# A fourth output buffer, and the last output bank copied in two halves

## The chip, the core and the metric

The kernel runs on one core of a Trainium2 chip. The metric is device time in microseconds (us), lower is better. TensorE (PE) multiplies matrices and writes into the accumulator memory PSUM, which has eight banks; VectorE (DVE), ScalarE (ACT) and GpSimd (POOL) do the elementwise work out of the on-chip buffer SBUF; SyncE (SP) issues all DMA transfers, in program order.

## The reference

A block-causal attention, then two gated feed-forward layers, the second of them fed by the first:

```python
attn = softmax(mask(q @ k.T / sqrt(64))) @ v          # 4 batches, 8 heads, 576 tokens, 64 wide
x = attn, heads joined                                # 2304 x 512
h = maximum(maximum(x @ w1, x @ w2), x @ w3)          # 2304 x 768
x = h @ w_out                                         # 2304 x 512
gate = sigmoid(x @ w_gate); val = x @ w_val           # 2304 x 1536 each
out = (gate * val) @ w_out2                           # 2304 x 512
```

## The kernel before

Each operand of a product is split into a high and a low part, and a product is three matmuls (high x high, high x low, low x high). Attention and layer one run first, interleaved by a planner, and write their result to a DRAM tensor `x2d`. Layer two then runs in three chunks `c` of 768 tokens. A chunk loads its part of `x2d` as `xraw` (L1107), forms seven combinations of its blocks (differences `t`, L1117; high parts `xc` cast on ScalarE, L1121; low parts subtracted by VectorE, L102), and multiplies them with seven combinations of weights by a Strassen-like scheme: seven products per block `n` of 128 hidden columns.

The weights of a block come in three parts, `x`, `y` and `z`, each loaded as `wr` (L1156), cast to its high part `wgx`, `wgy`, `wgz` on ScalarE (L1160), and subtracted to its low part on VectorE or GpSimd (L102). In chunk 0 the low part is also stored (`lowp`, L1167) for the later chunks. The products of a block (L1221 to L1223) go to three accumulator banks a, b, c in the order 0 (a), 5 (b), 4 (c), then 1 (a again, on `wgz`) and so on. Between product 0 and product 1, ScalarE copies bank a to `p1`, which VectorE adds to other products; product 1 then adds into that bank.

After twelve blocks, the output matmuls (L1275 to L1277) fill six banks per chunk, 128 tokens each. `leave(c, i)` copies bank `i` to an output buffer `osb` (ScalarE L93, VectorE L97, in the pattern A, A, V) and stores it. There are three output buffers, so bank `i` uses the buffer of bank `i - 3` and waits for its store.

What sets the order: the code gives each step a time `t` and a scheduler places the instructions of DVE, ACT, POOL and SP, by these and by when data and buffers become ready; PE's order is written out. The buffers of layer two reuse the memory of the phases before: the pools are laid one behind the other from the start of SBUF. A tile must then wait for the last use of whatever lay at its addresses. Layer one's pools, from the same start, are XT (26,624 B per partition), `raw` (four buffers of 4,096 B, weight preparation), `tmp` (four of 2,048 B, the running maximum `m`, L543 and L545), and so on. Layer two's pools begin like this:

```python
    wr_p = pool("wr", 4)      # 4 x 3,072 B
    hidden(2)                 # 2 x 6,144 B
    ost_p = pool("ost", 3)    # 3 x 2,048 B
    xr_p = pool("xr", 1)      # xraw, 12,288 B
    pt_p = pool("pt", 17)
```

Of the kernel before, what the change touches and what calls it, by code (L numbers as in the profile page):

```python
# [23 lines left out]
TOK = B * S  # L24
# [54 lines left out]
def block_attention_moe_moe(ctx: ExitStack, tc, kq1, v1, kq2, vt, wa, wb, out):  # L79
    nc = tc.nc  # L80
    wide = wa.dtype == U64
    V, A, G, T = nc.vector, nc.scalar, nc.gpsimd, nc.tensor
# [8 lines left out]
    def copy(e, out, in_, scale=None):  # L91
        if e == "A":
            A.activation(out, in_, AF.Copy, scale=scale) if scale is not None else A.copy(out, in_)  # L93
        else:
            n = V if e == "V" else G
            if scale is None:
                n.tensor_copy(out, in_)  # L97
            else:
                n.tensor_scalar(out=out, in0=in_, scalar1=scale, scalar2=None, op0=ALU.mult)  # L99
# [962 lines left out]
    def pool(name, bufs, **kw):  # L1062
        return ctx.enter_context(tc.tile_pool(name=name, bufs=bufs, reuse_waits="tile", **kw))

    HC = 2 * N2
    HID = []

    def hidden(n):
        p = pool(f"hid{len(HID)}", 1)
        HID.extend(p.tile([128, 2, HC], F32R, name=f"hid{len(HID) + k}") for k in range(n))  # L1070
# [7 lines left out]

    wr_p = pool("wr", 4)
    hidden(2)  # L1080
    ost_p = pool("ost", 3)
    xr_p = pool("xr", 1)
    pt_p = pool("pt", 17)
    wg_p = pool("wg", 2)
# [123 lines left out]
    WG, OW, OUTB, LAST, ASKED = {}, {}, {}, {}, {}  # L1208
# [71 lines left out]
    def leave(c, i):  # L1280
        def g():
            o = ost_p.tile([128, 512], F32, tag="ost", name="osb")
            copy(ENG["oc"][i % 3], o, OUTB[c, i])
            r0 = HC * c + 128 * i
            nc.sync.dma_start(out=out[r0 : r0 + 128, :], in_=o)
        return g

# [139 lines left out]
```

## Time and profile before

| | us |
|---|---|
| median of 3 runs | 893.38 |
| lowest and highest | 892.27 and 895.14 |
| the profiled execution, its own time | 895.03 |
| its span, first to last instruction | 892.9 |
| TensorE busy | 870.0 |
| VectorE, ScalarE, GpSimd busy | 582.0, 446.0, 96.4 |

All times in the rows below count from the span's start. Busy times of TensorE overlap a little, since matmuls are pipelined. The span is the time from the first to the last instruction; what lies around it is 2.1 us.

### The profile page before, as it was taken

How to read it: one execution, taken by the hardware profiler on the slowest of the kernel's cores; microseconds unless marked ns; L12 is line 12 of the kernel's file. 1: busy time of each engine (PE TensorE's matmuls, PEld its weight loads, DVE VectorE, ACT ScalarE, POOL GpSimd, SP SyncE). 2: the span in 40 equal slices, each digit the busy share in tenths (PEclk: the TensorE clock that was granted, in tenths of full speed). 3: DMA queues.
4: the chain of work that ended last, by engine and by line, in shares of the span. 5: the costliest groups of instructions: out<-in, count | busy, mean ns of one | idle time of the engine just before them, and what ended most of it. 6: DMA issues, size and time to landing. Idle time of an engine off the chain costs nothing.

```text
span 892.9 us, 15107 instructions
## 1 busy us (share of the span) xinstructions
PE 870.0 (97%) x5432; PEld 789.6 (88%) x5432; DVE 582.0 (65%) x1367; ACT 446.0 (50%) x1014; POOL 96.4 (11%) x91
## 2 busy tenths in 40 slices
PE   5899999999999999999999999999999999999997
PEld 4688889887998898889999999889999988999986
DVE  7999959996799699698354778821555711555400
ACT  7897646553464355345224655512566622565311
POOL 0000000000000000000002544200222300232300
PEclk9999999999999999999999999999999999999999
DMA  9921254346534444626317988744789844788232
GB/s 334 377 82 46 74 182 145 111 141 210 193 103 142 148 135 139 207 88 223 112 35 233 323 256 296 294 156 150 249 268 305 296 131 139 249 257 286 93 106 82
DMA packets 82810, 165.09 MB, mean 185 GB/s; under 512 B 10800, under 2 KB 23600, under 8 KB 82736
## 3 DMA queue, kind: packets, MB, share of 16 engines
q1 hardware_dynamic: 82736, 164.14, 55.6%
q8 instruction: 42, 0.69, 0.3%
q14 instruction: 32, 0.26, 0.1%
HBM read 126.35 MB, written 37.75 MB: 184 GB/s over the span
## 4 chain that ended last, share of the span: by engine, by line
PE 85%; DMA 7%; DVE 3%; SPq 2%; issue 1%; ACT 1%; POOL 1%; ACTq 0%; POOLq 0%; DVEq 0%
PE ps_m L535 9%; PE ps_m L537 8%; PE ps_m L536 8%; PE acc L1221 7%; PE acc L1222 7%; PE acc L1223 7%; PE acc L1276 5%; PE acc L1277 5%; PE acc L1275 5%; PE ps_o L488 5%; PE ps_t L452 4%; PE ps_s L376 3%; PE ps_m L574 2%; PE ps_m L576 2%; PE ps_m L575 2%; DMA qk<-in_kq_dram 2%
## 5 line engine op out<-in xcount | busy, mean ns | idle before, releaser
L535 PE MATMUL ps_m<-XT,w 128*128 128x320 f32 (+2 forms) x504 | 163.6, 325 | 2.7 <-DVE x2s L97 2.6
L537 PE MATMUL ps_m<-XT,w 128*128 128x320 f32 (+2 forms) x504 | 157.9, 313 | 0.3 <-DVE w L102 0.3
L536 PE MATMUL ps_m<-XT,w 128*128 128x320 f32 (+2 forms) x504 | 157.8, 313 | 0.1
L535 PEld LDWEIGHTS ps_m<-XT,w 128*128 128x128 f32 x504 | 95.0, 188 | 10.7 <-issue 3.5
L537 PEld LDWEIGHTS ps_m<-XT,w 128*128 128x128 f32 x504 | 94.9, 188 | 3.4 <-DVE w L102 0.5
L536 PEld LDWEIGHTS ps_m<-XT,w 128*128 128x128 f32 x504 | 95.1, 189 | 2.7 <-DVE XT L102 0.3
L400 ACT ACTIVATE E<-ps_s,nm 128x256 f32<-128x256 f32 (+3 forms) x128 | 66.4, 527 | 39.1 <-PE ps_t L452 31.2
L1277 PE MATMUL acc<-ow,hid 128*128 128x512 f32 x216 | 84.1, 390 | 0.0
L1276 PE MATMUL acc<-ow,hid 128*128 128x512 f32 x216 | 84.1, 390 | 0.0
L1275 PE MATMUL acc<-ow,hid 128*128 128x512 f32 x216 | 84.0, 389 | 0.0
L1223 PE MATMUL acc<-xc,wgx 128*128 128x384 f32 x216 | 72.2, 334 | 0.0
L1221 PE MATMUL acc<-xc,wgx 128*128 128x384 f32 x216 | 72.2, 334 | 0.0
L1222 PE MATMUL acc<-xc,wgx 128*128 128x384 f32 x216 | 72.2, 334 | 0.0
L97 DVE COPY osb<-acc 128x512 f32<-128x512 f32 x6 | 4.2, 692 | 95.8 <-PE acc L1277 88.8
L1189 ACT CAST ow<-or 128x512 fp32r<-128x512 f32 x36 | 22.4, 621 | 77.7 <-PE acc L1277 55.1
L1234 DVE TENSOR_TENSOR u<-acc,p 128x384 f32<-128x384 f32 x72 | 39.9, 554 | 30.3 <-PE acc L1223 22.9
L545 DVE TENSOR_TENSOR m<-ps_m,m 128x320 f32<-128x320 f32 (+2 forms) x84 | 41.7, 496 | 23.3 <-PE ps_m L537 21.9
L395 DVE TENSOR_REDUCE nm<-ps_s 128x1 f32<-128x256 f32 (+3 forms) x128 | 55.0, 472 | 2.2 <-ACT E L400 2.2
L452 PE MATMUL ps_t<-ident,E 128*128 128x128 f32 x320 | 45.6, 281 | 7.8 <-DVE E L99 4.2
L102 POOL TENSOR_TENSOR wgx<-wr,wgx 128x768 fp32r<-128x768 f32 x1 | 1.9, 1854 | 468.1 <-ACT wgx L1160 468.1
L1234 DVE TENSOR_TENSOR u<-acc,u 128x384 f32<-128x384 f32 x72 | 40.0, 556 | 16.7 <-PE acc L1223 15.5
L1221 PE MATMUL acc<-xc,wgy 128*128 128x384 f32 x144 | 48.6, 337 | 1.8 <-DVE u L1234 1.7
(122 smaller groups left out, 2080.4 us busy)
## 6 DMA issues: line engine op xcount, KB each, us to landing
praw<-in_wb_dram SPq DMA_DIRECT2D x36, 512.0 KB, 4.7
wr<-pairs SPq DMA_DIRECT2D x72, 256.0 KB, 3.7
wr<-pairs SPq DMA_DIRECT2D x36, 384.0 KB, 4.5
or<-outs SPq DMA_DIRECT2D x36, 256.0 KB, 3.5
wgx<-lowp SPq DMA_DIRECT2D x24, 384.0 KB, 4.0
wland<-in_wa_dram SPq DMA_DIRECT2D x5, 1536.0 KB, 16.4
qk<-in_kq_dram SPq DMA_DIRECT2D x16, 480.0 KB, 3.4
wgz<-lowp SPq DMA_DIRECT2D x24, 256.0 KB, 4.2
```

Source lines behind the costliest of these rows:

```text
L400: A.activation(E[h][:, e : e + 128 * (t + 1)], j.s[h, t], AF.Exp, bias=j.nm[:, c : c + 1], scale=1.0, accum_out=j.sm[:, c : c + 1],)
L452: T.transpose(ps[:, 128 * i : 128 * i + 128], E[h][:, e : e + 128], ident)
L535: T.matmul(ps, wt[:, 0, w, k], xh[:, k], start=(k == 0), stop=False)
L536: T.matmul(ps, wt[:, 0, w, k], xl[:, k], start=False, stop=False)
L537: T.matmul(ps, wt[:, 1, w, k], xh[:, k], start=False, stop=(k == KD - 1))
L1221: T.matmul(ps, w[:, 0, h], x[:, 0, h], start=start and h == 0, stop=False, skip_group_check=True)
L1222: T.matmul(ps, w[:, 0, h], x[:, 1, h], start=False, stop=False, skip_group_check=True)
L1223: T.matmul(ps, w[:, 1, h], x[:, 0, h], start=False, stop=h == 1, skip_group_check=True)
L1234: V.tensor_tensor(out=o, in0=BK[c, n, b][:, :N2], in1=x, op=ALU.add)
L1275: T.matmul(ps, h[:, 0, ct], w[:, 0], start=(f == 0), stop=False)
L1276: T.matmul(ps, h[:, 0, ct], w[:, 1], start=False, stop=False)
L1277: T.matmul(ps, h[:, 1, ct], w[:, 0], start=False, stop=(f == NF2 - 1))
```

## The change

The pool of output buffers gets a fourth buffer. For the last bank of the last chunk, the copy is made in two halves of 256 columns, the first on ScalarE and the second on VectorE, each with a store of its own in place of one store of 512 columns.

```diff
-    ost_p = pool("ost", 3)
+    ost_p = pool("ost", 4)
...
     def leave(c, i):
         def g():
             o = ost_p.tile([128, 512], F32, tag="ost", name="osb")
+            r0 = HC * c + 128 * i
+            if c + 1 == TOK // HC and i == 5:
+                for e, k in (("A", 0), ("V", 256)):
+                    copy(e, o[:, k : k + 256], OUTB[c, i][:, k : k + 256])
+                    nc.sync.dma_start(out=out[r0 : r0 + 128, k : k + 256], in_=o[:, k : k + 256])
+                return
             copy(ENG["oc"][i % 3], o, OUTB[c, i])
-            r0 = HC * c + 128 * i
             nc.sync.dma_start(out=out[r0 : r0 + 128, :], in_=o)
```

The order in which the instructions stand changes in the middle of the program too. On SyncE, where layer one ends and layer two begins (numbers in names are those of the buffers' tiles, `x2d` stores are the last results of layer one):

```order
-L1107 DMA xraw_5940<-x2d_72 128x4x768
 L595 DMA x2d_72<-x2s_5453 128x128
 L595 DMA x2d_72<-x2s_5453 128x64
@@ -220,4 +219,5 @@
 L1156 DMA wr_5945<-pairs0_73 128x768
 L1156 DMA wr_5949<-pairs0_73 128x512
+L1107 DMA xraw_5940<-x2d_72 128x4x768
 L1156 DMA wr_5953<-pairs0_73 128x512
 L1156 DMA wr_5967<-pairs1_74 128x768
```

The load of `xraw` has moved from among the stores of an earlier group to behind the first two weight loads of layer two.

On ScalarE at the same place, before (`m` and HR belong to layer one, `wgx_5960`, `wgz_5965` and `wgy_5974` to block 0, `wgx_5989`, `wgz_5993` and `wgy_5999` to block 1):

```order
L558 CAST HR_730<-m2_5781 128x320
L1160 CAST wgx_5960<-wr_5945 128x768
L1160 CAST wgz_5965<-wr_5949 128x512
L1160 CAST wgy_5974<-wr_5953 128x512
L1121 CAST xc6_5902<-t3_5985 128x768
L1160 CAST wgx_5989<-wr_5967 128x768
L1305 COPY p1_6014<-acc_6005 128x384
L1246 ACTIVATE c11_6049<-acc_6005 128x384
L1160 CAST wgz_5993<-wr_5976 128x512
```

and of the change:

```order
L1121 CAST xc1_5928<-xraw_5940 128x768
L1160 CAST wgx_5960<-wr_5945 128x768
L1160 CAST wgz_5965<-wr_5949 128x512
L1160 CAST wgy_5974<-wr_5953 128x512
L1121 CAST xc2_5930<-xraw_5940 128x768
L1121 CAST xc3_5929<-t4_5969 128x768
L1160 CAST wgx_5989<-wr_5967 128x768
L1160 CAST wgz_5993<-wr_5976 128x512
L1121 CAST xc6_5902<-t3_5985 128x768
L1160 CAST wgy_5999<-wr_5982 128x512
L1310 COPY p1_6014<-acc_6005 128x384
```

All `xc` casts have moved from among layer one's work to behind the last HR cast (`warm`, `xc0`, `xc4` and `xc5` stand just ahead of these rows), and the copy to `p1` now stands behind the casts of `wgz_5993` and `wgy_5999`, which were behind it. On SyncE the load for `wgy_5999` is `wr_5982`; it stands behind the store of the low part of `wgz_5965`.

At the end of VectorE's program, with what each instruction waits for (DMAHW: a transfer; PE, Activation, DVE: that engine), before:

```order
L97 COPY osb_9730<-acc_9459 128x512 [waits DMAHW5_49,PE_49]
L97 COPY osb_9748<-acc_9494 128x512 [waits DMAHW7_49,DVE_49,PE_49]
```

and of the change:

```order
L97 COPY osb_9730<-acc_9459 128x512 [waits DMAHW3_49,DMAHW4_49,DMAHW0_49,PE_49]
L97 COPY osb_9748<-acc_9494 128x256 [waits DMAHW6_49,DMAHW3_49,Activation_49]
```

The last copy is half as wide, and waits for ScalarE where it waited for TensorE.

## Rows read from the trace of the kernel before

**Rows 1.** The page, part 1: TensorE's busy time and share.

```profile
PE 870.0 (97%) x5432; PEld 789.6 (88%) x5432; DVE 582.0 (65%) x1367; ACT 446.0 (50%) x1014; POOL 96.4 (11%) x91
```

**Rows 2.** Waits of PE from 476 us on: total us, times, longest.

```profile
PE acc L1221 <- DVE u L1234: 1.7, 3, 1.2
```

**Rows 3.** Timeline of PE at the seam: start, us, engine, instruction.

```profile
475.62 0.31 PE L576 MATMUL ps_m<-HR,w 128*128 128x320 f32 x1
475.76 0.34 PE L1221 MATMUL acc<-xc,wgx 128*128 128x384 f32 x1
...
478.89 0.33 PE L1221 MATMUL acc<-xc,wgz 128*128 128x384 f32 x1
```

**Rows 4.** Timeline of SP's issues, 405 to 482 us.

```profile
427.76 0.54 SPq L1107 DMA_DIRECT2D xraw<-x2d  x1
...
465.40 1.74 SPq L1156 DMA_DIRECT2D wr<-pairs  x4
...
478.32 0.38 SPq L1156 DMA_DIRECT2D wr<-pairs  x1
...
479.82 0.48 SPq L1156 DMA_DIRECT2D wr<-pairs  x1
```

**Rows 5.** Tile `xraw`: its three loads, issue to landing.

```profile
DMA to landing us min/median/max: 7.3/8.7/9.4
```

**Rows 6.** Timeline of DVE, 440 to 465 us (brackets: idle before, releaser).

```profile
440.43 0.95 DVE L1117 TENSOR_TENSOR t<-xraw 128x768 f32<-128x768 f32 x1
...
463.71 0.49 DVE L545 TENSOR_TENSOR m<-ps_m,m 128x320 f32<-128x320 f32 x1 [2.08 <-PE ps_m L537]
```

**Rows 7.** Timeline of ACT, 468 to 485 us.

```profile
468.53 0.83 ACT L1160 CAST wgx<-wr 128x768 fp32r<-128x768 f32 x1 [2.14 <-DMA wr<-pairs]
...
477.06 0.48 ACT L1305 COPY p<-acc 128x384 f32<-128x384 f32 x1 [4.46 <-PE acc L1223]
...
481.55 0.62 ACT L1160 CAST wgz<-wr 128x512 fp32r<-128x512 f32 x1 [0.93 <-DMA wr<-pairs]
...
484.44 0.62 ACT L1160 CAST wgy<-wr 128x512 fp32r<-128x512 f32 x1 [1.33 <-DMA wr<-pairs]
```

**Rows 8.** Timeline of POOL at the seam.

```profile
469.45 1.85 POOL L102 TENSOR_TENSOR wgx<-wr,wgx 128x768 fp32r<-128x768 f32 x1 [468.15 <-ACT wgx L1160]
471.26 1.30 POOL L102 TENSOR_TENSOR wgz<-wr,wgz 128x512 fp32r<-128x512 f32 x1
```

**Rows 9.** Timeline of POOL, 703 to 710 us.

```profile
703.20 1.02 POOL L102 TENSOR_TENSOR hid<-u,hid 128x384 fp32r<-128x384 f32 x1 [2.31 <-issue]
...
707.92 1.73 POOL L102 TENSOR_TENSOR hid<-u,hid 128x384 fp32r<-128x384 f32 x1
```

**Rows 10.** Timeline of DVE, the same stretch.

```profile
707.12 1.66 DVE L1117 TENSOR_TENSOR t<-xraw,t 128x768 f32<-128x768 f32 x1
```

**Rows 11.** The page, part 6: loads, KB each, median us to landing.

```profile
wr<-pairs SPq DMA_DIRECT2D x72, 256.0 KB, 3.7
```

**Rows 12.** PE by stretch: us, busy (x), granted clock, DMA share, GB/s.

```profile
21.00:21.50 0.50, 0.41 (x2) 0.50 1.06 418
...
24.00:24.50 0.50, 0.50 (x6) 0.95 1.03 410
```

**Rows 13.** Timeline of PE after a gap early on.

```profile
21.09 1.54 PE L452 MATMUL ps_t<-ident,E 128*128 128x128 f32 x6 [2.21 <-ACT E L93]
```

**Rows 14.** Timeline of ACT at the end.

```profile
887.66 1.29 ACT L93 COPY osb<-acc 128x512 f32<-128x512 f32 x2 [1.48 <-PE acc L1277]
```

**Rows 15.** Timeline of DVE at the end.

```profile
889.14 0.69 DVE L97 COPY osb<-acc 128x512 f32<-128x512 f32 x1 [2.18 <-DMA out_dram<-osb]
```

**Rows 16.** Timeline of PE at the end: the last matmul.

```profile
887.89 0.39 PE L1277 MATMUL acc<-ow,hid 128*128 128x512 f32 x1
```

**Rows 17.** ACT by line and shape: count, busy us, mean ns, idle before.

```profile
L543 ACT COPY m<-ps_m 128x256 f32<-128x256 f32 x12 | 4.5, 374 | 1.7 <-PE ps_m L537 1.7
```

**Rows 18.** DVE by line and shape.

```profile
L97 DVE CAST XT<-ps_o 128x256 fp32r<-128x256 f32 x10 | 4.2, 420 | 0.3 <-PE ps_o L488 0.3
```

## The prediction

> **What bounds the kernel now.** I first read the totals of the page and the engines' shares: TensorE is busy for 870.0 of the 892.9 us [rows 1], so only what delays TensorE, or follows its last matmul, counts. Then the waits of TensorE from 476 us on: all that is left there is 1.7 us in three waits [rows 2]. From the seam between the two layers to the end TensorE thus has almost no slack, and a delay at the seam reaches the end nearly whole. The change touches two places, the tail and, by way of the memory layout, the seam.
>
> The seam in TensorE's timeline: its last matmul of layer one starts at 475.62, the first product of layer two follows at 475.76 with no gap, and the fourth product (the first on `wgz`) starts at 478.89 [rows 3]. In SyncE's timeline the load `xraw` is issued at 427.76, 48 us ahead, and four `wr` loads at 465.40 [rows 4].
>
> **The memory layout.** In the code, `xraw` begins at 26,624 B (XT) plus the room left after it: `wr` 12,288 + two hidden tiles 12,288 + three output buffers 6,144 = 30,720, and ends at 43,008. That is exactly where the four raw buffers of layer one (4 x 4,096 after XT) end. With a fourth output buffer it begins and ends 2,048 higher and so also covers the first of layer one's `tmp` buffers, which holds a maximum `m`. The order excerpts show what follows: the load is now issued behind the first two `wr` loads. The buffer's last reader is a max that starts at 463.71 [rows 6]; the `wr` loads in front wait for the last matmul on XT and start at 465.40.
>
> **The price of the seam, step by step.** T is the time at which `xraw` has landed.
>
> 1. Four issues take 1.74 us [rows 4], so the third stands at 465.40 + 2 x 0.435 = 466.3. From issue to landing it took 7.3, 8.7 and 9.4 us [rows 5]. With 640 KB of loads in front and as much behind I take the middle row: T = 475.0 (bounds 473.6 and 475.7).
> 2. ScalarE, before, had done the `xc` casts long ahead and cast the weights at once (468.53). Now `warm` and the casts of `xc0`, `xc4`, `xc5` and `xc1` stand in front of `wgx`, and all of these need `xraw`. `warm` and `xc0` lie beside VectorE's first difference, which takes 0.95 [rows 6] and which `xc4` needs; from there come four casts of 0.83, the duration of the weight cast of the same size [rows 7], the last being `wgx`: T + 4.3.
> 3. GpSimd subtracts for `wgx` and then `wgz`: 1.85 + 1.30 = 3.15 us when alone [rows 8]. Before, VectorE was nearly idle then; now it makes its row of `xc` subtractions at the same time. Later in the kernel, where both do that, a GpSimd subtraction of 384 columns takes 1.73 instead of 1.02 [rows 9], and a VectorE one 1.66 [rows 10] instead of 0.95. I take the factor 1.7, since this is the same pair of instructions: 5.35 us, T + 9.65. Bounds: 3.15 and 5.35.
> 4. SyncE stores the low part of `wgz`, and only then issues the load `wr` for `wgy` of the second block: its issues are 0.5 apart (three steps from 478.32 to 479.82 [rows 4]), T + 10.15.
> 5. The load lands 3.7 us later by the page's median for 256 KB [rows 11]; bounds 3.2 (478.32 to 481.55) and 4.6 (479.82 to 484.44) [rows 4, 7]. T + 13.85.
> 6. ScalarE casts it (0.62) and only then copies `p1` (0.48) [rows 7], which stands behind it in its order now and stood ahead of it before. T + 14.95. The fourth product adds into the bank that this copy reads, so it waits for it, and all of TensorE behind it.
>
> The first three products are hidden in this: they need `wgx` from GpSimd (T + 4.3 + 1.85 x 1.7 = T + 7.4) and take 3.1 us. The fourth starts at 475.0 + 14.95 = 489.95 in place of 478.89: **+11.1 us**. The second block's `p1` copy stands behind one more load, for the third block's `wgz`. That is issued when the second block's low parts have been stored, some 1.0 us after step 5, at about T + 14.9; with 3.7 + 0.62 + 0.48 the copy is done at T + 19.7. TensorE wants it six products later, at T + 14.95 + 6 x 1.04 = T + 21.2 (1.04 is a third of the 3.13 us between the first and the fourth product [rows 3]). Nothing is added, with 1.5 us in hand.
>
> The Trainium skill, "SBUF — State Buffer" (section on the two separate sides of SBUF), says that a VectorE instruction with two SBUF inputs and a GpSimd one reading SBUF take a shared port by turns, whole instruction by whole instruction. By it GpSimd's two subtractions would each wait for one VectorE instruction, an estimate of 3.15 + 2 x 0.95 = 5.05 against 5.35 by the rows; the sum would be 0.3 lower.
>
> **The clock.** TensorE now stands still before the first product, before its third matmul, and for some 4.5 us before the fourth product. At the start of the kernel, behind a gap of 2.21 us that ends at 21.09, the granted clock is at half (1.2 of 2.4 GHz), and it is back just after 24.0 [rows 12, 13]: 2.95 us of work at half speed, 1.5 us lost. I take that once, after the longest gap: **+1.5** (bounds 0, and 3.0 for two such stretches).
>
> **The tail.** The copy of bank 3 starts at 887.66 and that of bank 5 at 889.14, both held by the store of the buffer that they use [rows 14, 15]; the last matmul starts at 887.89 and takes 0.39, ending at 888.28 [rows 16]. With four buffers bank 3 starts when its matmul ends, bank 4 takes its place at 887.66 (store 0), and bank 5 can start when store 1 lands: the second of the two ScalarE copies now starts there, at 887.66 + 1.29 - 0.59 = 888.36. The halves: ScalarE 0.37, VectorE 0.42 by 256-column rows [rows 17, 18]. The order shows that VectorE's half waits for ScalarE and no longer for TensorE itself: the halves go one behind the other, 888.4 + 0.37 + 0.06 + 0.42 = 889.25 against 889.14 + 0.69 = 889.83 before. The extra store's issue lies under the second half. **-0.6** (bounds -0.4 and -1.0, the latter if the halves ran together).
>
> The Trainium skill, "PSUM — Partial Sum Buffer" (section on bank collisions), forbids two engines in one bank at once, even on separate columns. It speaks against the split: two engines then bring only smaller pieces. The order agrees; by a reading that let them overlap, the tail would give 1.0.
>
> **Sum.** +11.1 + 1.5 - 0.6 = +12.0. On the profiled execution's own times: span 892.9 to 904.9, 895.0 to 907.0 us. That execution is 1.65 above the median of the runs; on the median, 893.4 + 12.0 = 905.4 us.
>
> **The rivals.**
>
> *Quick seam.* The same chain at its low ends: T = 473.6, GpSimd undisturbed (3.15), the load in 3.2, no loss of clock. 473.6 + 4.3 + 3.15 + 0.5 + 3.2 + 1.1 = 485.85, +7.0; 893.4 + 7.0 - 0.6 = 899.8. For it: the DMA engines are little used at the seam before; against it: the contention rows. The 1.7 us of [rows 2] could also come back, since the loads get a lead over TensorE: 898.1.
>
> *A second hold.* If the loads of the second block take 1.5 us longer than reckoned, its `p1` copy holds TensorE as well, and the clock falls twice: +11.1 + 3.0 + about 2 - 0.6, 909.
>
> *Covered load.* The transfer stays hidden and only the tail counts: 893.4 - 0.6 = 892.8, no slower. For that the fourth product must start by 482.2 (478.89 + 2.7 + 0.6), so T must be near 467 by the chain above, under 1 us after the issue; no row for this size is below 7.3. The change's own purpose, two halves at once, is the other thing that may not happen, and is in the tail's bounds.
>
> **Chances and range.** Forecast (902 to 908) 0.62; quick seam 0.23; second hold 0.12; covered load 0.03. Some 0.3% (2.7 us) is what a measurement of this kernel can tell from no change; only the last case lies inside it: faster 0.01, same 0.02, slower 0.97. The range 899.0 to 908.5 leaves out the last case, the lower end of the quick one and the upper half of the second hold.
>
> **What would show it.** `xraw` issued near 466.3 and landed near 475; no `xc` cast on ScalarE before that; gaps of TensorE at 475.8 and before the first `wgz` matmul near 490; GpSimd's `wgx` subtraction near 3 us; `p1` behind a `wgy` cast; a clock at half after it; the tail's last store issued near 1.0 us after the last matmul's end where it was 1.6. I am wrong if TensorE starts the second layer without a gap, or if most of a gap there is made up by 560 us.

## The result, and the profile after

The changed kernel takes 905.67 us (median of 4 runs, 904.77 to 906.85) where the kernel before takes 894.26 (4 runs beside it): a ratio of 1.0123, 95% interval 1.0107 to 1.0139. It is slower by 11.4 us; 905.4 was predicted.

Its profiled execution has a span of 903.2 us (905.29 in all), 10.3 more than that of before. Its layer one ended earlier, though, by 1.77 us (last layer-one matmul at 473.85 instead of 475.62), so that 12.1 us were lost behind that point. The layout does not explain the earlier end: in the kept traces it falls between 473.7 and 477.6 with the new layout and between 474.7 and 476.2 with the old one. Times of the two traces are compared by their distance from the start of that last matmul.

TensorE's waits from 476 us on (total us, times, longest), which answer to [rows 2]:

```profile
PE acc L1221 <- ACT wgx L1160: 4.6, 1, 4.6
PE acc L1221 <- ACT p L1310: 3.3, 1, 3.3
PE acc L1221 <- DVE u L1234: 1.3, 1, 1.3
PE acc L1223 <- POOL wgx L102: 0.9, 1, 0.9
```

Three of the four are new. TensorE's timeline at the seam shows where they stand ([rows 3] before):

```profile
473.85 0.31 PE L576 MATMUL ps_m<-HR,w 128*128 128x320 f32 x1
...
478.81 0.69 PE L1221 MATMUL acc<-xc,wgx 128*128 128x384 f32 x1 [4.65 <-ACT wgx L1160]
...
480.76 0.69 PE L1223 MATMUL acc<-xc,wgx 128*128 128x384 f32 x1 [0.95 <-POOL wgx L102]
...
489.57 0.57 PE L1221 MATMUL acc<-xc,wgz 128*128 128x384 f32 x1 [3.32 <-ACT p L1310]
```

The fourth product starts 15.72 us behind the last matmul of layer one, where it was 3.27: +12.45. SyncE's timeline ([rows 4] before):

```profile
463.63 0.80 SPq L1156 DMA_DIRECT2D wr<-pairs  x2
464.52 0.54 SPq L1107 DMA_DIRECT2D xraw<-x2d  x1
...
483.09 0.38 SPq L1156 DMA_DIRECT2D wr<-pairs  x1
```

Tile `xraw`, issue to landing ([rows 5] before; the first of its three loads took 9.9):

```profile
DMA to landing us min/median/max: 9.2/9.9/9.9
```

The load now stands behind two `wr` loads, which wait for the end of the matmuls on XT, and lands at T = 474.47, 0.6 us behind the start of TensorE's last matmul and 0.3 behind its end (473.85 + 0.31). What follows on ScalarE, in its timeline ([rows 7] before):

```profile
474.47 0.21 ACT L1139 ACTIVATE warm<-xraw 128x8 f32<-128x8 f32 x1 [8.55 <-DMA xraw<-x2d]
...
477.93 0.83 ACT L1160 CAST wgx<-wr 128x768 fp32r<-128x768 f32 x1
...
483.51 0.83 ACT L1121 CAST xc<-t 128x768 fp32r<-128x768 f32 x1 [2.98 <-DVE t L1117]
...
487.79 0.83 ACT L1121 CAST xc<-t 128x768 fp32r<-128x768 f32 x1 [2.19 <-DVE t L1117]
488.52 0.61 ACT L1160 CAST wgy<-wr 128x512 fp32r<-128x512 f32 x1
489.04 0.47 ACT L1310 COPY p<-acc 128x384 f32<-128x384 f32 x1
```

VectorE's timeline in the same stretch ([rows 6, 10] before):

```profile
478.94 2.58 DVE L102 TENSOR_TENSOR xc<-xraw,xc 128x768 fp32r<-128x768 f32 x1
481.45 2.02 DVE L1117 TENSOR_TENSOR t<-xraw,t 128x768 f32<-128x768 f32 x1
...
485.74 2.02 DVE L1117 TENSOR_TENSOR t<-xraw 128x768 f32<-128x768 f32 x1
```

And GpSimd's ([rows 8] before):

```profile
478.83 1.87 POOL L102 TENSOR_TENSOR wgx<-wr,wgx 128x768 fp32r<-128x768 f32 x1 [477.53 <-ACT wgx L1160]
480.67 1.98 POOL L102 TENSOR_TENSOR wgz<-wr,wgz 128x512 fp32r<-128x512 f32 x1
...
485.67 1.27 POOL L102 TENSOR_TENSOR wgz<-wr,wgz 128x512 fp32r<-128x512 f32 x1 [3.01 <-ACT wgz L1160]
```

Read backwards from the fourth product: it waits for the `p1` copy (489.04), which stands behind the `wgy` cast and the cast of `xc6`; that one waits 2.19 us for VectorE's difference `t3`, which ends at 487.76. The two casts behind it are not held by a load: the chain is VectorE's. There three subtractions that take 0.95 elsewhere took 2.58, 2.02 and 2.02, each while GpSimd was in a subtraction. This was no accident of one execution: in the five kept traces that have the new layout and GpSimd's part in it (the changed kernel twice, the 64 B of padding and the extra matmuls twice, below), the three take 2.57 to 2.58, 2.02 to 2.03 and 2.01 to 2.04.

The granted clock by stretch (us, busy, clock, DMA share, GB/s; [rows 12] before):

```profile
476.00:476.50 0.50, 0.00 (x0) 0.57 0.47 134
...
478.00:478.50 0.50, 0.00 (x0) 0.50 0.00 0
...
486.00:486.50 0.50, 0.24 (x1) 0.69 0.80 117
...
489.00:489.50 0.50, 0.00 (x0) 1.00 0.47 136
489.50:490.00 0.50, 0.43 (x2) 0.73 0.33 75
490.00:490.50 0.50, 0.50 (x3) 0.50 0.56 178
...
493.00:493.50 0.50, 0.50 (x5) 0.86 1.07 410
```

It is at half (1.2 of 2.4 GHz) twice: from 476.1, during the first stand-still, to 486.3, and from 489.7 to 493.1. The first stretch lies inside the hold: its three products end at 486.2, before the fourth may start at 489.57. The second costs 0.13 + 6 x 0.25 + 0.07 = 1.7 us, half of the time spent at the lower clock.

The end: TensorE's last matmul in its timeline ([rows 16] before):

```profile
898.82 0.39 PE L1277 MATMUL acc<-ow,hid 128*128 128x512 f32 x1
```

ScalarE's copies there ([rows 14] before):

```profile
897.88 1.78 ACT L93 COPY osb<-acc 128x512 f32<-128x512 f32 x3 [0.77 <-PE acc L1277]
```

VectorE's half ([rows 15] before):

```profile
899.69 0.42 DVE L97 COPY osb<-acc 128x256 f32<-128x256 f32 x1 [1.80 <-ACT osb L93]
```

SyncE's issues of the two halves' stores:

```profile
899.68 0.86 SPq L1287 DMA_DIRECT2D out_dram<-osb  x2
```

From the start of the last matmul to the end of the span it is 903.2 - 898.82 = 4.38 us, before 892.9 - 887.89 = 5.01: the tail gained 0.63. VectorE's half starts where ScalarE's three copies end.

The account: +12.45 at the fourth product and +1.7 by the clock make 14.15; from block 1 to block 12 the starts of the blocks show 1.4 of it made up, and the tail gives 0.63. That is 12.1, as the spans say. The 1.4 belongs to these two executions: from block 1 to block 12 it is 134.2 us in the trace of before and 132.8 here, but 133.3 to 135.6 over the six kept traces with the old layout, and 133.7 in the second profile of the changed kernel.

### The profile page after: what moved, and what is told of

The parts are those of the page before. It is cut to its first block, busy times and chain, and to the rows that moved or that the text cites. A ratio compares the mean times of both kernels' runs of the same rounds, so it can differ in the third digit from the quotient of the medians.

```text
span 903.2 us, 15114 instructions
## 1 busy us (share of the span) xinstructions
PE 876.2 (97%) x5432; PEld 795.9 (88%) x5432; DVE 587.1 (65%) x1367; ACT 447.2 (50%) x1015; POOL 97.1 (11%) x91
## 4 chain that ended last, share of the span: by engine, by line
PE 87%; DMA 5%; DVE 3%; issue 2%; POOL 1%; ACT 1%; SPq 0%; DVEq 0%; ACTq 0%; POOLq 0%
PE acc L1221 9%; PE ps_m L535 8%; PE acc L1223 8%; PE acc L1222 8%; PE ps_m L537 8%; PE ps_m L536 8%; PE acc L1276 5%; PE acc L1277 5%; PE acc L1275 5%; PE ps_o L488 5%; PE ps_t L452 4%; PE ps_s L376 4%; PE ps_m L574 2%; DMA qk<-in_kq_dram 2%; PE ps_m L576 2%; PE ps_m L575 2%
## 5 line engine op out<-in xcount | busy, mean ns | idle before, releaser
L1221 PE MATMUL acc<-xc,wgx 128*128 128x384 f32 x216 | 73.5, 340 | 4.6 <-ACT wgx L1160 4.6
L1223 PE MATMUL acc<-xc,wgx 128*128 128x384 f32 x216 | 73.5, 340 | 0.9 <-POOL wgx L102 0.9
L1222 PE MATMUL acc<-xc,wgx 128*128 128x384 f32 x216 | 73.3, 339 | 0.0
L97 DVE COPY osb<-acc 128x512 f32<-128x512 f32 (+1 forms) x6 | 3.9, 648 | 94.1 <-PE acc L1277 90.3
L1221 PE MATMUL acc<-xc,wgz 128*128 128x384 f32 x144 | 48.9, 340 | 3.3 <-ACT p L1310 3.3
```

Source lines behind the costliest of these rows:

```text
L1221: T.matmul(ps, w[:, 0, h], x[:, 0, h], start=start and h == 0, stop=False, skip_group_check=True)
L1222: T.matmul(ps, w[:, 0, h], x[:, 1, h], start=False, stop=False, skip_group_check=True)
L1223: T.matmul(ps, w[:, 1, h], x[:, 0, h], start=False, stop=h == 1, skip_group_check=True)
```

## The experiments

**The layout alone.** Three buffers and one copy as before, with 64 B of unused memory in front of `xraw`:

```diff
     ost_p = pool("ost", 3)
+    pool("pad", 1).tile([128, 16], F32, name="pad")
     xr_p = pool("xr", 1)
```

> This is the kernel before, with three output buffers and one last copy, and 64 B per partition of unused memory in front of the buffer of xraw. Theory (the memory layout alone makes the seam): any shift of xraw upwards puts it over the first tmp buffer of layer one, so xraw is issued behind the first two wr loads, lands about 10 us later, TensorE's fourth product starts about 15 us after that landing, the clock falls, and the run takes about 12.1 to 12.6 us more than before (the change's 11.4 plus the 0.6 of its better tail): about 906.5 us, ratio 1.0135. Rival (the fourth buffer or the halves themselves cost the time): no delay at the seam, within 0.2% of before.

Measured: 906.58 us against 894.59, ratio 1.0133 (1.0112 to 1.0154). The load is issued at 464.36, behind two `wr` loads, and the fourth product (L1222 here, one line lower) starts 14.5 us behind layer one's last matmul (473.69):

```profile
488.21 0.69 PE L1222 MATMUL acc<-xc,wgz 128*128 128x384 f32 x1 [3.86 <-ACT p L1306]
```

The landing is at 473.11, so the product starts at T + 15.1, to a tenth the changed kernel's distance. 64 B do what a whole buffer does: neither buffer nor halves are needed for the loss.

**The halves alone.**

```diff
-    ost_p = pool("ost", 4)
+    ost_p = pool("ost", 3)
```

(from the changed kernel, the halves kept)

> This is the kernel before with the halves alone: three output buffers, the last bank copied in two halves with two stores. Theory: the seam is as before; the halves still wait for the store of the buffer that they use and go one behind the other, 0.37 + 0.06 + 0.42 = 0.85 against one VectorE copy of 0.69, so the end comes 0 to 0.3 us later: ratio within 0.3% of 1. Rival (the halves do the change's harm): about +11 us, 905. Rival (the halves run at once): 0.2 to 0.3 us earlier, and VectorE's half starts with ScalarE's.

Measured: 894.7 against 894.59, ratio 1.0001 (0.9987 to 1.0015). ScalarE's half in its timeline:

```profile
887.62 0.37 ACT L93 COPY osb<-acc 128x256 f32<-128x256 f32 x1 [0.17 <-DMA out_dram<-osb]
```

VectorE's half:

```profile
888.02 0.42 DVE L97 COPY osb<-acc 128x256 f32<-128x256 f32 x1 [2.56 <-ACT osb L93]
```

ScalarE's half is held by the store of the buffer, VectorE's by ScalarE's half; the tail is 5.02 us (last matmul at 886.38, span 891.4), as before. The harm isn't theirs, and with three buffers there is no gain either.

**GpSimd taken out of the seam.** In the changed kernel, the low parts of the weights of blocks 0 and 1 go to VectorE:

```diff
         box = {}
+        if c == 0 and n < 2:
+            low = "V"
```

> This is the changed kernel with all low parts of the weights of blocks 0 and 1 of chunk 0 subtracted on VectorE and none of them on GpSimd. Theory A (at the seam VectorE stood still while GpSimd subtracted, and VectorE's row is what TensorE's fourth product waits for): the xc and t subtractions during that time take 0.95 again in place of 2.58, 2.02 and 2.02; 3.7 us are saved, 0.87 + 0.60 + 0.60 are added to VectorE's row, so the fourth product starts some 1.2 to 1.8 us sooner after the landing of xraw (about 13.5 in place of 15.1 us), and the run takes about 904.2 us, -0.15 to -0.2% of the changed kernel. Theory B (the chain of the prediction: both engines slow each other by 1.7, and the load for wgy of the second block comes last): the store of the low part of wgz and the load behind it move with VectorE's row, and the fourth product comes 1 to 3 us later, 907 to 909.

Measured: 904.28 against 894.59, ratio 1.0117 (1.0094 to 1.0140). VectorE's same two subtractions now (landing at 478.15):

```profile
482.62 0.95 DVE L102 TENSOR_TENSOR xc<-xraw,xc 128x768 fp32r<-128x768 f32 x1
...
484.36 0.95 DVE L1117 TENSOR_TENSOR t<-xraw,t 128x768 f32<-128x768 f32 x1
```

ScalarE's timeline ahead of the fourth product:

```profile
490.50 0.62 ACT L1162 CAST wgy<-wr 128x512 fp32r<-128x512 f32 x1 [0.51 <-DMA wr<-pairs]
491.03 0.47 ACT L1312 COPY p<-acc 128x384 f32<-128x384 f32 x1
```

TensorE's fourth product:

```profile
491.55 0.67 PE L1223 MATMUL acc<-xc,wgz 128*128 128x384 f32 x1 [2.32 <-ACT p L1312]
```

The load for `wgy` of the second block, in SyncE's timeline:

```profile
486.36 0.38 SPq L1158 DMA_DIRECT2D wr<-pairs  x1
```

The fourth product starts at T + 13.4 in place of T + 15.1: theory A, with the 13.5 it gave. And once VectorE's row is short, what ends last is the prediction's own chain: that load, issued at 486.36 and landed at 490.50 (4.1 us). The time alone would not have told: the two ratios' intervals overlap, as 1.7 us is about what a measurement of this kernel can miss.

**The fourth buffer out of the way.** Four buffers and the halves, the fourth behind all other pools, used by bank 3:

```diff
-    ost_p = pool("ost", 4)
+    ost_p = pool("ost", 3)
...
-    combos((0, 4, 5, 1, 3, 2))
+    combos((0, 4, 5, 1, 3, 2)); ost2_p = pool("ost2", 1)
...
-            o = ost_p.tile([128, 512], F32, tag="ost", name="osb")
+            o = (ost2_p if i == 3 else ost_p).tile([128, 512], F32, tag="ost", name="osb")
```

> This has four output buffers and the halves, but the fourth buffer (used by bank 3 of every chunk) lies behind all other buffers of layer two, so that xraw keeps its place. Theory: the seam is that of before (xraw issued 48 us ahead, no gap of TensorE, the clock up), and the tail keeps its gain of 0.6: the last instruction about 4.0 us after the end of the last matmul where it was 4.6; about 893.7 where before takes 894.3, ratio 0.9993, within 0.3% of 1. Rival (the shift is not the cause): about 905.

Measured: 894.23 against 894.59, ratio 0.9995 (0.9984 to 1.0006). The seam has no gap; layer one ends at 476.15 and the first product follows:

```profile
476.29 0.34 PE L1221 MATMUL acc<-xc,wgx 128*128 128x384 f32 x1
```

The tail is 892.5 - 888.09 = 4.41 us: the gain of 0.6 is there, and too small for the times to show.

**The same without halves** (`ost2_p` as above in the kernel before):

> This has the fourth output buffer behind all others (used by bank 3) and no halves: bank 5 is copied whole by VectorE. Theory (all of the tail's gain is the fourth buffer's, and the halves, which go one behind the other, give nothing back): VectorE's copy starts when the last matmul ends and takes 0.69, so the last store is issued 0.75 us after the last matmul's end, where the version with the halves has about 0.95 and before 1.6; the end comes 0.0 to 0.2 us sooner than with the halves, about 4.2 to 4.4 us from the start of the last matmul to the end of the span in place of 5.0; about 893.7 where before takes 894.4, within 0.3%. Rival (the halves give part of the gain, as the smaller last store lands sooner): 4.5 to 4.8 us.

Measured: 894.24 against 895.14, ratio 0.9993 (0.9981 to 1.0004). VectorE's whole copy of bank 5:

```profile
888.71 0.69 DVE L97 COPY osb<-acc 128x512 f32<-128x512 f32 x1 [1.42 <-PE acc L1277]
```

It starts 0.1 us behind the end of the last matmul (888.21 + 0.39); the tail is 892.5 - 888.21 = 4.29, 0.1 shorter than with the halves. All of the gain is the buffer's. This is the best tail of the runs; as a whole kernel it isn't shown to beat the one before.

**What holds VectorE's half.** The two halves in different buffers, first in that of bank 3:

```diff
                 for e, k in (("A", 0), ("V", 256)):
+                    o = (ost2_p if k else ost_p).tile([128, 512], F32, tag="ost", name="osb") if k else o
                     copy(e, o[:, k : k + 256], OUTB[c, i][:, k : k + 256])
```

> This is the version with the fourth buffer behind all others, and with the two halves of bank 5 in two different buffers. Theory (the accumulator bank makes VectorE's half wait): VectorE's half still starts where ScalarE's ends, within 0.1 us, and the tail is as with one buffer, about 4.4 us. Rival (the shared output buffer makes it wait): both halves start together and the tail is 0.3 to 0.4 us shorter.

It told nothing on this: VectorE's half waited for bank 3's store, which still held that buffer, to 890.60; its one run took 895.83. Then with a small buffer of its own (`ost2_p` for bank 3 as before):

```diff
-    combos((0, 4, 5, 1, 3, 2))
+    combos((0, 4, 5, 1, 3, 2)); ost2_p = pool("ost2", 1); half_p = pool("half", 1)
...
+                for e, k, d in (("A", 0, o[:, :256]), ("V", 256, half_p.tile([128, 256], F32, name="half"))):
+                    copy(e, d, OUTB[c, i][:, k : k + 256])
+                    nc.sync.dma_start(out=out[r0 : r0 + 128, k : k + 256], in_=d)
```

> This is the version with the fourth buffer behind all others; VectorE's half of bank 5 goes to a small buffer of its own that nothing else uses (in the earlier run it shared the buffer of bank 3 and waited for that one's store). Theory (the accumulator bank makes VectorE's half wait): it still starts within 0.1 us of the end of ScalarE's half, and the end of the span stands about 4.4 us behind the start of the last matmul. Rival (the shared output buffer makes it wait): both halves start together, and that stretch is about 4.0.

ScalarE's copies at the end (the third of them is its half):

```profile
885.49 1.78 ACT L93 COPY osb<-acc 128x512 f32<-128x512 f32 x3 [0.77 <-PE acc L1277]
```

VectorE's half:

```profile
887.31 0.42 DVE L97 COPY half<-acc 128x256 f32<-128x256 f32 x1 [1.80 <-ACT osb L93]
```

It starts 0.04 after ScalarE's end (887.27), and the tail is 890.8 - 886.43 = 4.37 (one run, 892.73). What the halves share is now only the accumulator bank, and the trace still names ScalarE's half as what VectorE's waited for. For the change, the order excerpt shows that such a wait stands in the program; what two engines would do in one bank at once wasn't tried.

**The clock.** TensorE's gap ahead of the fourth product filled with 18 matmuls, into the bank that block 1 overwrites:

```diff
-            if start:
+            if start and (c, n, b) not in BK:
                 BK[c, n, b] = bank()
             ps = BK[c, n, b][:, :N2]
+            if c == 0 and n == 0 and k == 1:
+                BK[0, 1, "a"] = bank()
+                for _ in range(18):
+                    T.matmul(BK[0, 1, "a"][:, :N2], WG[0, 0, "x"][:, 0, 0, :128], XC[0][:, 0, 0], start=True, stop=True, skip_group_check=True)
```

> This is the changed kernel with 18 extra matmuls of 384 columns between the third and the fourth product of block 0, into a bank that the next block overwrites; they fill TensorE's gap ahead of the fourth product and read only what the first product has read. Theory (the second stretch at half clock, behind that gap, costs 1.7 us): the granted clock stays at 1.0 from about 486 us on, the second row of products takes 1.7 us less, and the run takes about 1.7 us less than the changed kernel: 903.9, ratio to before 1.011. Rival (TensorE waits for VectorE's row behind the fourth product anyway, so the lost clock is hidden): the clock stays up, but new waits on VectorE take its place, and the time is that of the changed kernel within 0.5 us, 905.4.

Measured: 907.56 against 895.14, ratio 1.0127 (1.0107 to 1.0148), no less than the changed kernel (1.0123), though the theory's 1.011 lies inside the interval too. At the seam the clock did what was expected (1.00 from 487 on), but a wait near block 9 was 2.9 us where the changed kernel has 1.3:

```profile
557.63 0.45 PE L1225 MATMUL acc<-xc,wgy 128*128 128x384 f32 x1 [2.94 <-DVE u L1238]
```

Behind that wait the clock fell once more, from 558.5 to 562.0, which costs another 1.7 us by the same count; behind the changed kernel's wait of 1.3 it stays at 1.00.

```profile
559.00:559.50 0.50, 0.50 (x3) 0.50 0.72 66
```

So it was run again, beside the changed kernel on the same chip:

> This is the kernel with 18 extra matmuls ahead of the fourth product once more, beside the changed kernel on the same chip. Theory A (the 1.1 us that the kept clock gives at the seam are lost again where the loads of chunk 0 bound, near block 9, because TensorE only gets there sooner): the wait near block 9 is again 1 to 2 us longer than the changed kernel's 1.3, and both run within 0.15% of each other. Theory B (that wait was a late transfer of one execution): the wait is 0.8 to 1.4, and the run takes 1.0 to 1.7 us less than the changed kernel.

> The changed kernel itself, beside the one with the extra matmuls: 905.7, and a wait of 0.8 to 1.4 us near block 9 as in its first profile. If that wait is 2 to 3 us here, it varies by execution and says nothing of the extra matmuls.

Measured: 905.0 with the extra matmuls, ratio 1.0104 (1.0087 to 1.0120); 907.33 without them, 1.0131 (1.0108 to 1.0153). The clock by stretch at the seam, with them:

```profile
490.00:490.50 0.50, 0.26 (x2) 1.00 0.45 131
...
492.50:493.00 0.50, 0.50 (x5) 1.00 1.03 359
```

The wait near block 9 in TensorE's timeline, with them:

```profile
556.73 0.44 PE L1225 MATMUL acc<-xc,wgy 128*128 128x384 f32 x1 [1.84 <-DVE u L1238]
```

And without them:

```profile
557.61 0.44 PE L1221 MATMUL acc<-xc,wgy 128*128 128x384 f32 x1 [1.32 <-DVE u L1234]
```

From the landing of `xraw` to the start of block 1 it is 18.85 us in both executions of the changed kernel, and 17.7 in both with the extra matmuls: the kept clock gives 1.15 us there, not 1.7, the rest going into short gaps before the next product. Near block 9, longer waits stand against that: 0.5 us in the second run, and 1.6 in the first, with the 1.7 of the fallen clock on top. Neither theory holds as put. The wait of 1.84 lies between the two, and the second run took 2.3 us less than the changed kernel beside it (0.26%), more than either theory allows, with overlapping intervals. How much of the 1.15 a run keeps stays open, since the two timings differ by more (+12.4 and +9.6 us over before).

## Why the prediction was right, point by point

**The cause.** The prediction put the loss on the layout. 64 B of padding alone give it, and the fourth buffer elsewhere doesn't: shown.

**Step 1, T.** The issue came at the predicted place (0.89 us behind the first `wr` load; 466.3 - 465.4 predicted). The landing took 9.9 instead of 8.7 us, above the upper bound, which was 9.4; in the six executions that have the shift the first load took 8.7 to 10.5. This mis-sized term is +1.2 here; with the new layout T itself lies from 0.6 before to 1.2 us behind the start of the last matmul of layer one (0.6 before was predicted), so the size of this term differs by execution.

**Step 2, ScalarE.** `wgx` was cast by 478.76, T + 4.3, as predicted.

**Step 3, the engine that pays.** This is the step that failed. A factor of 1.7 was put on GpSimd, 5.35 us. GpSimd took from 478.83 to 482.65, 3.8 us; the predicted sign, a `wgx` subtraction near 3 us, is absent (1.87). VectorE paid, 2.58 + 2.02 + 2.02 in place of 3 x 0.95, 3.8 us more. The rows show turns: GpSimd's first subtraction begins 0.11 ahead of VectorE's and runs its 1.87 undisturbed; VectorE's ends 0.82 after it, about its 0.95 alone; GpSimd's second ends 1.13 after that; VectorE's next ends 0.82 after that. The Trainium skill, "SBUF — State Buffer" (section on who interferes with whom), says just this of a VectorE instruction with two SBUF inputs and a GpSimd one that reads SBUF: whoever issues first has the shared port for the whole instruction and the other stands still. The trace agrees. The estimate from it in the prediction, 5.05, took VectorE to be first both times; with GpSimd first it is 1.85 + 0.95 + 1.30 = 4.1, an estimate too, against 3.8 measured. That the two collide and that taking GpSimd away frees VectorE is shown by the third experiment.

**Steps 4 to 6, the last chain.** With GpSimd quicker, the load for `wgy` was issued at T + 8.6, not T + 10.15; with the 4.1 us of the third experiment and 1.1 for cast and copy it would have let the fourth product start at about T + 13.9. VectorE's row came 1.2 us later: `t3`, `xc6`, `wgy`, `p1`. So T + 15.1 (the same to 0.03 in the five traces named above) met the predicted T + 14.95 by another way, and that is luck: a GpSimd cost put too high stood in for a VectorE cost that the chain did not have. The ScalarE order (`p1` behind `xc6` and `wgy`), which step 6 named, was right.

**The sum.** At the fourth product +12.45 against +11.1, of which 1.2 is the landing. Clock +1.7 against +1.5, though twice at half, the first time hidden. Tail -0.63 against -0.6, with the halves one behind the other as argued. Against these excesses of 1.5 stand 1.4 us made up by block 12: the kernel before loses 1.55 us in blocks 4 to 7 against an even 7.28 a block, the changed one nothing there, while both have the wait near block 9 and the same pace from 560 us on. The prediction had named this under its quick-seam rival, at 1.7, and left it out of its sum. The loads' lead over TensorE as its reason was argued, not tested, and the 1.4 itself varies by execution. So 12.0 was right in total with errors of about +1.5 and -1.4 in its terms, which cancelled by luck; the layout, the order of events at the seam and the size of the loss were foreseen, the engine that pays was not.

**Rivals.** The quick seam fails by its T (2.0 us before the start of the last matmul of layer one, where the earliest seen is 0.6) and by VectorE's 3.8 us, which it does not have; its GpSimd, 3.15, was nearer to the measured 3.8 than the forecast's 5.35. The second hold did not come: no wait of TensorE stands between the fourth product and block 9. The covered load is out.

## What to carry to other kernels

Before a buffer count is changed, work out whose memory each later pool then covers: 64 B moved the issue of a load from 48 us ahead of the end of layer one to 9 us ahead of it (464.36 to 473.69), so that it landed when TensorE needed its results, and 12 us followed, where the edit's own gain was 0.6. Put such a buffer behind the others, or where nothing new is covered. Where two engines are put side by side, ask which of them goes first and which one the next wait depends on, not only by what factor the pair slows down.

## What was not expected of the hardware

VectorE's subtraction with two operands in SBUF was stretched from 0.95 to 2.58 us by a GpSimd subtraction of 1.87 that began 0.11 ahead of it, while GpSimd lost nothing in its first. And TensorE's clock fell to half twice within 20 us, the second time after a stand-still of 3.3 us that followed some 6.5 us of work, all of it at half; with the gap filled it stayed at 1.00 there. Behind a later wait it fell again in one trace (2.9 us) and not in three others (1.3, 1.3 and 1.8 us).
